# Half of the exchange of probabilities issued from SyncE, y's stores behind it in program order, and the last tile's sums of y put off

## The chip, the cores and the metric
One core of a Trainium2 chip. The time is device microseconds of one execution, the median of several runs; 1285.63 us for the kernel before. A profiled execution gives the trace; its own time is given beside it.

## The reference
Three stages follow each other over 4608 tokens of width 512. Names in brackets are those of the kernel.

```python
# 1. attention in chunks of 64 tokens, 8 heads of 64
p = exp(scores - max(scores)); p /= sum(p) + 1e-9      # scores = scale * qc @ kc.T   [sc, p]
x = p @ vc                                             # [x], split into [xh] + [xl]
# 2. FFN, 512 -> 2048 -> 512
h = x @ w_in; g = h * cos(h); y = g @ w_out            # [h], [gh]+[gl], [y]
# 3. FFN, 512 -> 1024 -> 512
h2 = y @ w_in2; s = h2 * softmax(h2)
ln = (s - mean(s)) / sqrt(var(s) + 1e-6) * g_ln
out = ln @ w_out2                                      # [o]
```

Inputs are float32; w_in, w_out, w_in2 and w_out2 arrive as 64-bit floats and are converted on the chip.

## The kernel before
Float32 products are made of three products of rounded halves (hi x hi, lo x hi, hi x lo), so operands are kept in pairs such as xh and xl, whi and wlo.

**Steps.** Stage 2 runs over 9 tiles of 512 tokens and 16 slices of the hidden width: 144 steps. A step n has 12 matmuls `h<-...` of slice n and 12 matmuls `y<-...` of slice n - 2. Steps 34 to 127 are written out in one order for every engine by `step(n)`; between their fixed parts stand slots ("e", "p1", "y", "a1", "d1", "a2", "d2", "p2") into which tables put the other work: p slots are for TensorE, a for ScalarE (ACT), d for VectorE (DVE).

**Attention inside the steps.** While tile t is worked on, the attention of tile t + 1 is made in two units of 256 tokens, the first begun two steps ahead of the tile's own steps, the second eight steps later. The table `exchanged` places a unit's parts by step and slot: DVE transposes q and k (`qt`, `kt`), TensorE makes the scores (`sc<-kt,qt`), DVE takes maximum, difference, sum and quotient, ACT the exponential. Then the probabilities have to be transposed in 64 x 64 blocks: DVE transposes 32 x 32 blocks (`ptr<-p`, line 545) and 16 DMAs of 32 KB put the blocks into their places (`ptb<-ptr`, line 552). This is the exchange; its DMAs are issued by GpSimd (POOL). TensorE then multiplies with v (`x<-ptb,vi`), at the end of the unit's step 8, ahead of the `h` matmuls of step 9, and `att_x` splits x into xh and xl.

**Weights of stage 3.** They are converted inside the steps too, by the pieces that `conv_at`, `blk_sum`, `keep` and `keep_out` place: loads `st<-in_moe_w...`, conversion in `z` (one buffer), and stores to DRAM (`w2f<-z`, `w2_..`).

**y.** At a tile's end y is moved out of PSUM (`ye<-y`), four sums of its quadrants are formed (`ts`, `sum_y`; stage 3's first product is a Strassen-Winograd one with seven products), and six DMAs `yd<-ye`, `yd<-ts` store both (`store_y`). `load_y(i)` loads pair i (256 tokens) again as `yr`, `split_y` makes `yh` (ACT) and `yl` (DVE) of it. Loads `yr`, `ye`, `ts` and the weights' loads share a pool "st" of two buffers.

**Stage 3** takes 18 pairs. The first three are mixed into the end of stage 2; from pair `EARLY` = 3 on a loop is written out in order: pair i's products `h2` (seen as `h<-whi,yh`), the softmax and the norm of pair i - 1, DVE transposes `bt`, 16 DMAs `lt<-bt` per tile, the split into `lh` and `ll`, and the products `o<-whi,lh` for 128 tokens at a time.

**What sets the order.** TensorE, ACT and DVE follow the written order in steps 34 to 127 and in the last loop. On SyncE (SP) only calls through the wrapper `sync` can be kept in program order, and only in the first 24 steps, where `in_order_loads` is true; elsewhere a scheduler puts SP's DMAs in the order in which it expects their operands.

Of the kernel before, what the change touches and what calls it, by code (L numbers as in the profile page):

```python
# [11 lines left out]
F32 = mybir.dt.float32  # L12
# [17 lines left out]
def kernel(  # L30
# [12 lines left out]
    nc = tc.nc  # L43
# [4 lines left out]
    P = 128  # L48
# [182 lines left out]

    def load_w2in(g):
        t = sp_.tile([P, 1024], U64, tag="st", name="st")
        nc.sync.dma_start(out=t, in_=w_in2[g * P:(g + 1) * P, :])
        raw["in2", g] = t

    def load_w2out(g):

        t = sp_.tile([P, 1024], U64, tag="st", name="st")
        for c in range(4):  # L240
            nc.sync.dma_start(
                out=t[32 * c:32 * (c + 1)].rearrange("p (e m) -> p e m", e=2),
                in_=w_out2.rearrange("(c q p) m -> c p q m", c=4, p=32)[c, :, 2 * g:2 * g + 2],
            )
        raw["out2", g] = t
# [4 lines left out]
    def conv(key, e, k):  # L250
        t = raw[key]
        w = t[:, HALVES[e]].bitcast(I32).rearrange("p (c w) -> p c w", w=2)
        low, high = w[:, :, 0], w[:, :, 1]
        if k == 0:
            if e == 0:
                wz[key] = zp.tile([P, 1024], I32, tag="z", name="z")
            act.activation(out=low, in_=low.bitcast(U32), func=AF.Copy, scale=2.0 ** -29)
            act.activation(out=wz[key][:, HALVES[e]].bitcast(F32), in_=high.bitcast(F32), func=AF.Abs)
            return
        z = wz[key][:, HALVES[e]]  # L260
        zf = z.bitcast(F32)
        if k == 1:
            dve.tensor_scalar(out=zf, in0=zf, scalar1=TINY, scalar2=None, op0=ALU.max)
            dve.tensor_scalar(
                out=z, in0=z, scalar1=3, scalar2=0x3FFFFFFF,
                op0=ALU.logical_shift_left, op1=ALU.bitwise_and,
            )
            return
        dve.scalar_tensor_tensor(
            out=z, in0=high, scalar=-(1 << 30), in1=z, op0=ALU.bitwise_and, op1=ALU.bitwise_or  # L270
        )
        dve.tensor_tensor(out=z, in0=z, in1=low, op=ALU.add)
        if key[0] == "in2" and e == 1:
            kk, x = key[1] % 2, key[1] // 2
            raw.pop(key)
            nc.sync.dma_start(
                out=w2f[kk][:, 1024 * x:1024 * (x + 1)], in_=wz.pop(key).bitcast(F32)
            )

# [1 line left out]

    def load_blk(kk):
        t = sp_.tile([P, 2048], F32, tag="st", name="wf")
        nc.sync.dma_start(out=t, in_=w2f[kk])
        blk[kk] = t, zp.tile([P, 1024], F32, tag="z", name="z"), sp_.tile([P, 2048], F32R, tag="st", name="wk")

    def blk_part(kk):
# [11 lines left out]
    def keep(kk, e, key, half):  # L299
        parts = blk[kk][2][:, 1024 * e:1024 * (e + 1)]  # L300
        split(blk_part(kk)[key], parts[:, HALVES[0]], parts[:, HALVES[1]], half=half)
        if half == 1:
            nc.sync.dma_start(
                out=w2_dram[key].rearrange("p (x k c) -> p x k c", x=2, k=2)[:, :, kk],
                in_=parts.bitcast(F32).rearrange("p (x c) -> p x c", x=2),
            )

    def keep_out(g, e, half):
        parts = raw["out2", g].bitcast(F32R)
        hi, lo = parts[:, 0:1024], parts[:, 1024:2048]  # L310
        src, sl = wz["out2", g].bitcast(F32)[:, HALVES[e]], HALVES[e]
        mul = gcol[:, 2 * g + e:2 * g + e + 1]
        if half == 0:
            act.activation(out=hi[:, sl], in_=src, func=AF.Copy, scale=mul)
            return
        dve.scalar_tensor_tensor(
            out=lo[:, sl], in0=src, scalar=mul, in1=hi[:, sl].bitcast(F32), op0=ALU.mult, op1=ALU.subtract
        )
        if e == 1:
            raw.pop(("out2", g)), wz.pop(("out2", g))  # L320
            nc.sync.dma_start(out=w2_dram[g], in_=parts.bitcast(F32))

    def fetch_w2(key):
        hi, lo = wtile(F32R, "whi"), wtile(F32R, "wlo")
# [212 lines left out]
    def att_pt(i):  # L537
        p = pr.pop(i)
        x = UNITS[i][1] // 2 * HU
        if i >= EXCH:  # L540

            t = work(i, (4, x, 32), "t", "ptr")
            o = work(i, (4, x, 32), "t", "ptb")
            tc.keep_in_program_order(
                nc.vector.transpose(
                    out=t.rearrange("p g x s -> p x g s"),
                    in_=p.rearrange("p x r (h s) -> p x (r h) s", s=32),
                )
            )
            for g in range(4):  # L550
                for c in range(4):
                    nc.gpsimd.dma_start(  # L552
                        out=o[32 * g:32 * (g + 1), c].rearrange("p x s -> p (x s)"),
                        in_=t[32 * c:32 * (c + 1), g].rearrange("p x s -> p (x s)"),
                    )
            ptb[i] = o
            return
        if small(i):
            t = ps_h.tile([P, x, P], F32, tag="h", name="pt")
        else:  # L560
            t = ps_a.tile([P, x, P], F32, tag="a", name="pt")
        for y in range(x):
            pe.transpose(out=t[:, y], in_=p[:, y].rearrange("p r k -> p (r k)"), identity=ident)
        pt[i] = t
# [125 lines left out]
    def mm_out(n):  # L690
# [17 lines left out]
                pe.matmul(out=o, lhsT=wb, rhs=a, start=False, stop=last)  # L708
        if last and not PIN <= n + LAG < END:
            evac_y(j, f)  # L710
            if f == NF - 1:
                for e in range(4):
                    sum_y(j, e)
                store_y(j)
# [2 lines left out]

    def load_part(j):
        t = sp_.tile([P, KD, T], F32, tag="st", name="yp")
        nc.sync.dma_start(out=t.rearrange("p m t -> p (m t)"), in_=y_part[j])  # L720
        parts[j] = t

    ye = {}
# [1 line left out]
    def evac_y(j, f, half=None):  # L725
# [17 lines left out]
            return  # L743
        yps.pop(j), ye.pop(j)
        if f < NF - 1:
            nc.sync.dma_start(out=y_part[j], in_=s.rearrange("p m t -> p (m t)"))
            return

        ys[j] = s, sp_.tile([P, 8, 256], F32, tag="st", name="ts")
# [13 lines left out]
    def store_y(j):  # L763
        s, ts = ys.pop(j)
        for p in range(2):
            dst = y_dram[j][p].rearrange("p (x t) -> p x t", t=P)
            sl, sr = slice(p * P, (p + 1) * P), slice(256 + p * P, 256 + (p + 1) * P)
            nc.sync.dma_start(out=dst[:, 0:4], in_=s[:, :, sl])
            nc.sync.dma_start(out=dst[:, 4:6], in_=s[:, 2:4, sr])
            nc.sync.dma_start(out=dst[:, 6:14], in_=ts[:, :, sl])  # L770


    NPAIR = NI // 2
# [23 lines left out]
    if True:  # L797
# [70 lines left out]
        def load_next_v(i):  # L868
# [7 lines left out]
            (6, "early", att_ptc), (6, "late", att_pv), (6, "late", load_next_v), (7, "early", att_x),  # L876
        )
        exchanged = (
            (0, "d1", lambda i: att_tr(i, "q")), (0, "d2", lambda i: att_tr(i, "k")),
            (2, "p1", att_qk), (2, "p1", load_next),  # L880
            (2, "d1", att_max), (3, "d1", att_sub), (3, "a2", att_exp),
            (4, "d1", att_sum), (5, "d1", att_mul), (5, "d2", att_pt),
            (8, "p2", att_pv), (8, "p2", load_next_v),
            (9, "e", lambda i: att_x(i, 0)), (9, "e", lambda i: att_x(i, 1)),
        )
# [14 lines left out]
        for i in range(SUB, NU):  # L900
# [3 lines left out]
            elif j == 2:  # L904
                place(i, NF + (0 if o == 0 else NB - 1), wide)
            else:
                place(i, j * NF - NF + (-2 if o == 0 else 6), exchanged)

        def plan(n, when, what):
            att.setdefault((n, when), []).append((lambda i: what(), NU))  # L910
# [5 lines left out]
        for t in (2, 3):  # L916
            o = NF * t
            for x in range(2):
                plan(o + 5, "p2", lambda g=2 * x + t - 2: load_w2in(g))
            conv_at(("in2", t - 2), ((o + 6, "a2"), (o + 7, "d2"), (o + 8, "d2"), (o + 7, "a1"), (o + 9, "d2"), (o + 10, "d2")))  # L920
            conv_at(("in2", t), ((o + 12, "a2"), (o + 12, "d2"), (o + 13, "d1"), (o + 13, "a1"), (o + 13, "d2"), (o + 16, "d1")))
        for t in (4, 5):
            o, kk = NF * t, t - 4
            plan(o + 5, "p2", lambda kk=kk: load_blk(kk))
# [10 lines left out]
        for t in (6, 7):  # L935
# [2 lines left out]
                g = 2 * (t - 6) + x  # L938
                plan(o + 5, "p2", lambda g=g: load_w2out(g))
            g = 2 * (t - 6)  # L940
            conv_at(("out2", g), ((o + 6, "a2"), (o + 7, "d2"), (o + 8, "d2"), (o + 7, "a1"), (o + 9, "d2"), (o + 10, "d2")))
            conv_at(("out2", g + 1), ((o + 12, "a2"), (o + 12, "d2"), (o + 13, "d1"), (o + 13, "a1"), (o + 13, "d2"), (o + 16, "d1")))
            for x, n0, wa, wd in ((0, 12, "a1", "d1"), (1, 16, "a2", "d2")):
                for e in range(2):
                    plan(o + n0, wa, lambda g=g + x, e=e: keep_out(g, e, 0))
                    plan(o + n0, wd, lambda g=g + x, e=e: keep_out(g, e, 1))
# [211 lines left out]
        W2_STEPS = (2, 3, 5, 8, 9, 9, 10, 10, 11, 12)  # L1158
        late_w = [(w, g) for g in range(NB // 2, NF // 2) for w in ("in", "out")]

        SLOTS = "e", "p1", "y", "a1", "d1", "a2", "d2", "p2"

        def step(n):
            if n == PIN:
# [29 lines left out]
                    plan(n + d, when, lambda j=j: store_y(j))  # L1194

        for n in range(NSTEP + LAG + 1):
            in_order_loads[0] = n < NF + NB
            ordered[0] = False
            if PIN <= n < END:
                step(n)  # L1200
# [34 lines left out]
            rest = n - NSTEP + NF  # L1235
            if rest == 3:
                load_y(0)
            elif rest == 4:
                split_y(0)
            for key, when in zip(BLOCKS + tuple(range(NF2 // 2)), (3, 3, 5, 5, 6, 7, 7, 13, 13, 15, 15)):  # L1240
# [6 lines left out]


        LAG2 = 7
        load_y(EARLY + 1, nc.gpsimd)  # L1250
        ordered[0] = True
        for i in range(EARLY, NI // 2 + (LAG2 + 1) // 2 + 1):
            p, t = i - 1, 2 * i - LAG2
# [43 lines left out]
                blocks32(p, 0)  # L1297
            if new:
                pair_sum(i, 1)
            if i == EARLY:  # L1300
                split_y(i + 1)
            if old:
                blocks32(p, 1)
                if p % 2:
# [2 lines left out]
            if new:  # L1307
                pair_mm(i, 2)
            half_o(t + 1, 0)
            if EARLY < i and i + 1 < NPAIR:  # L1310
                split_y(i + 1)
            if new:
                pair_sum(i, 2)
# [4 lines left out]
            half_o(t + 1, 1)  # L1318
            if new:
                pair_sum(i, 3)  # L1320
            if i + 2 < NPAIR:
                load_y(i + 2)

# [26 lines left out]
```

## Time and profile before

| | before |
|---|---|
| median of 3 runs (lowest to highest) | 1285.63 us (1285.53 to 1288.3) |
| the profiled execution's own time | 1284.95 us |
| its span in the trace | 1283.2 us |
| mean granted TensorE clock | 0.992 |
| PE (TensorE) busy | 1246.1 us, 97% |
| DVE busy | 957.9 us, 75% |
| ACT busy | 834.5 us, 65% |
| POOL busy | 122.4 us, 10% |

TensorE is busy for 97% of the span; the other engines have room on the average. A change can gain by closing TensorE's gaps, 37 us in all, and it loses by opening new ones. Matmuls are pipelined: each 128x512 matmul is shown with 0.39 us, but they start 0.227 us apart.

### The profile page before, as it was taken

The numbers are of one execution on the slowest core, as the hardware profiler recorded it, in microseconds if no ns is written. First come the engines' busy times: TensorE is split into PE (matmuls) and PEld (weight loads), VectorE is DVE, ScalarE is ACT, GpSimd is POOL, SyncE is SP. The second block draws the span as 40 slices with busy tenths as digits, with TensorE's granted clock in tenths as the row PEclk, the third lists the DMA queues.
The fourth block names the chain that finished last, engine by engine and source line by source line (L and its number), as shares of the span: only waits on it lengthen the run. The fifth ranks groups of instructions, "written<-read, shape, count | busy, mean of one in ns | idle before, by whom it ended". The sixth has DMA issues, their size and how long they took to land.

```text
span 1283.2 us, 20464 instructions
## 1 busy us (share of the span) xinstructions
PE 1246.1 (97%) x7556; PEld 1008.9 (79%) x7556; DVE 957.9 (75%) x1556; ACT 834.5 (65%) x1243; POOL 122.4 (10%) x272
## 2 busy tenths in 40 slices
PE   5899999999999999999999999999999999999998
PEld 4667778888878878878878878888878888888886
DVE  5887989687777777777778878757788777777761
ACT  5777876576656666656667767657756656656552
POOL 0000000020120220120121122000000000000000
PEclk9999999999999999999999999999999999999999
DMA  8952344343352343543563461380475443554224
GB/s 240 218 118 84 113 132 108 81 148 62 73 160 55 65 133 94 127 124 90 129 148 66 117 148 42 115 299 29 144 203 150 119 119 103 136 143 124 68 63 109
DMA packets 247940, 153.95 MB, mean 120 GB/s; under 512 B 180000, under 2 KB 220448, under 8 KB 246048
## 3 DMA queue, kind: packets, MB, share of 16 engines
q1 hardware_dynamic: 241456, 145.30, 43.5%
q0 software_dynamic: 6288, 7.22, 2.3%
q8 instruction: 59, 0.97, 0.3%
q14 instruction: 41, 0.34, 0.1%
q10 hardware_dynamic: 96, 0.13, 0.0%
HBM read 85.73 MB, written 41.68 MB: 99 GB/s over the span
## 4 chain that ended last, share of the span: by engine, by line
PE 72%; DVE 10%; ACT 8%; DMA 4%; POOL 3%; issue 2%; SPq 1%; ACTq 0%; POOLq 0%; DVEq 0%
PE h L105 34%; PE y L105 21%; PE o L105 13%; POOL ptb L552 3%; DMA ptb<-ptr 3%; DVE z L105 2%; DVE r L105 2%; ACT r L105 2%; PE x L105 2%; PE sc L105 1%; DVE gl L105 1%; ACT kt L105 1%; ACT hs L105 1%; DMA yr<-yd 1%; ACT whi L105 1%
## 5 line engine op out<-in xcount | busy, mean ns | idle before, releaser
L105 ACT ACTIVATE r<-r 128x512 f32<-128x512 f32 x288 | 181.8, 631 | 144.0 <-DVE r L105 138.2
L105 PE MATMUL h<-xh,whi 128*128 128x512 f32 x576 | 230.4, 400 | 2.0 <-ACT xh L105 1.4
L105 PE MATMUL h<-xh,wlo 128*128 128x512 f32 x576 | 226.4, 393 | 0.0
L105 PE MATMUL h<-xl,whi 128*128 128x512 f32 x576 | 225.8, 392 | 0.0
L105 PE MATMUL y<-gl,whi 128*128 128x512 f32 x544 | 212.7, 391 | 0.5 <-DVE gl L105 0.3
L105 PE MATMUL y<-gh,whi 128*128 128x512 f32 x544 | 211.9, 392 | 0.8 <-ACT gh L105 0.7
L105 PE MATMUL y<-gh,wlo 128*128 128x512 f32 x544 | 211.9, 390 | 0.0
L105 DVE SCALAR_TENSOR_TENSOR r<-kt,hs 128x512 f32<-128x512 int32 x144 | 99.0, 687 | 88.3 <-ACT kt L105 85.7
L552 POOL DMA_DIRECT2D ptb<-ptr x192 | 94.5, 500 | 708.3 <-DVE r L105 309.3
L105 DVE SCALAR_TENSOR_TENSOR hs<-r,hs 128x512 f32<-128x512 f32 x136 | 92.8, 682 | 59.6 <-ACT r L105 59.3
L105 ACT ACTIVATE hs<-h 128x512 f32<-128x512 f32 x144 | 85.0, 591 | 77.1 <-PE h L105 68.9
L105 PEld LDWEIGHTS h<-xh,whi 128*128 128x128 f32 x576 | 108.8, 189 | 27.8 <-issue 2.5
L105 PEld LDWEIGHTS h<-xl,whi 128*128 128x128 f32 x576 | 108.8, 189 | 23.8 <-issue 1.4
L105 PEld LDWEIGHTS h<-xh,wlo 128*128 128x128 f32 x576 | 108.8, 189 | 23.5 <-issue 0.4
L105 PEld LDWEIGHTS y<-gh,whi 128*128 128x128 f32 x544 | 101.8, 188 | 23.9 <-ACT gh L105 1.9
L105 PEld LDWEIGHTS y<-gl,whi 128*128 128x128 f32 x544 | 102.1, 188 | 23.2 <-DVE gl L105 2.4
L105 PEld LDWEIGHTS y<-gh,wlo 128*128 128x128 f32 x544 | 102.1, 188 | 21.3 <-DVE wlo L105 0.3
L105 PE MATMUL o<-whi,lh 128*128 128x512 f32 x288 | 112.4, 390 | 1.3 <-ACT os L105 1.3
L105 PE MATMUL o<-wlo,lh 128*128 128x512 f32 x288 | 112.3, 390 | 0.0
L105 PE MATMUL o<-whi,ll 128*128 128x512 f32 x288 | 112.1, 389 | 0.0
L105 DVE TENSOR_TENSOR gl<-hs,gh 128x512 fp32r<-128x512 f32 x136 | 93.0, 684 | 10.4 <-ACT gh L105 10.3
L105 PE MATMUL h<-whi,yh 128*128 128x512 f32 x252 | 98.6, 391 | 1.6 <-ACT yh L105 1.6
(108 smaller groups left out, 2077.9 us busy)
## 6 DMA issues: line engine op xcount, KB each, us to landing
lt<-bt SPq DMA_DIRECT2D x144, 128.0 KB
yr<-yd SPq DMA_DIRECT2D x17, 896.0 KB
yd<-ts SPq DMA_DIRECT2D x18, 512.0 KB
out<-os SPq DMA_DIRECT2D x142, 64.0 KB
vi<-in_v SPq DMA_DIRECT2D x64, 128.0 KB
qi<-in_q SPq DMA_DIRECT2D x224, 32.0 KB
ki<-in_k SPq DMA_DIRECT2D x224, 32.0 KB
ptb<-ptr POOLq DMA_DIRECT2D x192, 32.0 KB, 1.7
```

What stands on the lines that cost most here:

```text
L105: ins = getattr(self.engine, name)(*args, **kwargs)
L552: nc.gpsimd.dma_start(out=o[32 * g:32 * (g + 1), c].rearrange("p x s -> p (x s)"), in_=t[32 * c:32 * (c + 1), g].rearrange("p x s -> p (x ...
```

## The change
Four things are changed together.

1. Of an exchange's 16 DMAs the 8 of the groups g < 2 are issued by SP, the other 8 by POOL as before.
2. In steps 34 to 127 SP keeps program order: `in_order_loads` is true there, and all stores and loads in them go through `sync`.
3. The table of slots: k's transpose goes one step later, the scores from slot p1 to p2 of step 2, the maximum from d1 to d2. The product with v of a tile's first unit (`first_x`) goes from the end of step 8 to slot p1 of step 9, that is behind the 12 `h` matmuls of step 9; the second unit's (`second_x`) stays. Pieces of the weights' conversion go up to some steps later, and slot p2 stands ahead of a2 and d2.
4. The last tile's four sums and its `store_y` go from the end of stage 2 to behind pair 3's last sums; pair 4's load goes from POOL, behind the loop of steps, to SP, right behind pair 3's load; pair 4's `split_y` goes behind the second transpose `bt` and the `ll` of that iteration.

```diff
@@ att_pt
-                    nc.gpsimd.dma_start(
+                    (sync if g < 2 else nc.gpsimd).dma_start(
                         out=o[32 * g:32 * (g + 1), c].rearrange("p x s -> p (x s)"),
@@ load_w2in, load_w2out, conv, load_blk, keep, keep_out, load_part, evac_y, store_y
-            nc.sync.dma_start(out=dst[:, 0:4], in_=s[:, :, sl])
+            sync.dma_start(out=dst[:, 0:4], in_=s[:, :, sl])
...
@@ mm_out
-            if f == NF - 1:
+            if f == NF - 1 and j < NJ - 1:
                 for e in range(4):
                     sum_y(j, e)
                 store_y(j)
@@ exchanged
-            (0, "d1", lambda i: att_tr(i, "q")), (0, "d2", lambda i: att_tr(i, "k")),
-            (2, "p1", att_qk), (2, "p1", load_next),
-            (2, "d1", att_max), (3, "d1", att_sub), (3, "a2", att_exp),
+            (0, "d1", lambda i: att_tr(i, "q")), (1, "d2", lambda i: att_tr(i, "k")),
+            (2, "p2", att_qk), (2, "p2", load_next),
+            (2, "d2", att_max), (3, "d1", att_sub), (3, "a2", att_exp),
             (4, "d1", att_sum), (5, "d1", att_mul), (5, "d2", att_pt),
+        )
+        first_x = (
+            (9, "p1", att_pv), (9, "p1", load_next_v),
+            (9, "a1", lambda i: att_x(i, 0)), (9, "d1", lambda i: att_x(i, 1)),
+        )
+        second_x = (
             (8, "p2", att_pv), (8, "p2", load_next_v),
             (9, "e", lambda i: att_x(i, 0)), (9, "e", lambda i: att_x(i, 1)),
@@ place
-                place(i, j * NF - NF + (-2 if o == 0 else 6), exchanged)
+                place(i, j * NF - NF + (-2 if o == 0 else 6), exchanged + (second_x if o else first_x))
@@ conv_at, as one example of four
-            conv_at(("in2", t), ((o + 12, "a2"), (o + 12, "d2"), (o + 13, "d1"), (o + 13, "a1"), (o + 13, "d2"), (o + 16, "d1")))
+            conv_at(("in2", t), ((o + 13, "a1"), (o + 13, "d1"), (o + 13, "d2"), (o + 13, "a2"), (o + 14, "d2"), (o + 16, "d1")))
@@
-        SLOTS = "e", "p1", "y", "a1", "d1", "a2", "d2", "p2"
+        SLOTS = "e", "p1", "y", "a1", "d1", "p2", "a2", "d2"
@@ the loop of steps
-            in_order_loads[0] = n < NF + NB
+            in_order_loads[0] = n < NF + NB or PIN <= n < END
...
+            elif rest == 16:
+                load_y(EARLY + 1)
@@ the loop of pairs
-        load_y(EARLY + 1, nc.gpsimd)
...
-            if i == EARLY:
-                split_y(i + 1)
             if old:
                 blocks32(p, 1)
...
-            if EARLY < i and i + 1 < NPAIR:
+            if i + 1 < NPAIR:
                 split_y(i + 1)
...
             if new:
                 pair_sum(i, 3)
+            if i == EARLY:
+                for e in range(4):
+                    sum_y(NJ - 1, e)
+                store_y(NJ - 1)
             if i + 2 < NPAIR:
                 load_y(i + 2)
```

On SP, around the stores of tile 2's y (`yd_82`), before:

```order
L105 DMA ki<-in_k 32x8x32 x16
L276 DMA w2f_115<-z 128x1024
L768 DMA yd_82<-ye 128x4x128
L769 DMA yd_82<-ye 128x2x128
L768 DMA yd_82<-ye 128x4x128
L769 DMA yd_82<-ye 128x2x128
L770 DMA yd_82<-ts 128x8x128 x2
L234 DMA st<-in_moe_w_in 128x1024 x2
```

And after, where `ptb<-ptr` are the 8 DMAs of the tile's first exchange:

```order
L105 DMA w2f_115<-z 128x1024
L105 DMA qi<-in_q 32x8x32 x16
L105 DMA ki<-in_k 32x8x32 x16
L105 DMA ptb<-ptr 32x256 x8
L105 DMA yd_82<-ye 128x4x128
L105 DMA yd_82<-ye 128x2x128
L105 DMA yd_82<-ts 128x8x128
L105 DMA yd_82<-ye 128x4x128
L105 DMA yd_82<-ye 128x2x128
L105 DMA yd_82<-ts 128x8x128
L105 DMA st<-in_moe_w_in 128x1024 x2
```

The 8 DMAs of the exchange now stand on SP ahead of all six stores of y and of the weights' load; the store of z stands ahead of the loads of q and k, where it stood behind them.

On TensorE, around the first unit's product with v (`x<-ptb,vi`), before:

```order
L105 MATMUL y<-gh,whi 128x512
L105 MATMUL y<-gl,whi 128x512
L105 MATMUL y<-gh,wlo 128x512
L105 MATMUL x<-ptb,vi 64x64 x32
L105 MATMUL h<-xh,whi 128x512
L105 MATMUL h<-xl,whi 128x512
L105 MATMUL h<-xh,wlo 128x512
```

And after:

```order
L105 MATMUL h<-xh,whi 128x512
L105 MATMUL h<-xl,whi 128x512
L105 MATMUL h<-xh,wlo 128x512
L105 MATMUL x<-ptb,vi 64x64 x32
L105 MATMUL y<-gh,whi 128x512
L105 MATMUL y<-gl,whi 128x512
L105 MATMUL y<-gh,wlo 128x512
```

The product has gone behind the 12 `h` matmuls that it stood ahead of.

On DVE, in the iteration of pair 3 (`h_8992`, `h_8993` are pair 2's rows, `h_92..` pair 3's, `yl` pair 4's lower half), before:

```order
L105 STREAM_TRANSPOSE bt<-h_8992 128x32x32
L105 TENSOR_TENSOR h_9243<-h_9262,h_9243 128x512
L105 TENSOR_TENSOR h_9242<-h_9262,h_9243 128x512
L105 TENSOR_TENSOR yl<-yr,yh 128x1024
L105 TENSOR_TENSOR yl<-yr,yh 128x768
L105 STREAM_TRANSPOSE bt<-h_8993 128x32x32
L105 TENSOR_TENSOR ll<-lt,lh 128x1024
```

And after:

```order
L105 STREAM_TRANSPOSE bt<-h_8992 128x32x32
L105 TENSOR_TENSOR h_9233<-h_9252,h_9233 128x512
L105 TENSOR_TENSOR h_9232<-h_9252,h_9233 128x512
L105 STREAM_TRANSPOSE bt<-h_8993 128x32x32
L105 TENSOR_TENSOR ll<-lt,lh 128x1024
L105 TENSOR_TENSOR yl<-yr,yh 128x1024
L105 TENSOR_TENSOR yl<-yr,yh 128x768
```

`yl` has gone behind the second transpose and `ll`. The last tile's four sums `ts` stood 17 to 23 rows ahead of this `yl`; now they stand 9 to 11 rows behind it.

## Rows read from the trace of the kernel before

**Rows 1.** Waits of PE, 240 to 940 us: total us, times, longest.

```profile
PE x L105 <- DMA ptb<-ptr: 10.0, 6, 2.8
```

**Rows 2.** PE's timeline: start us, us, engine line operation out<-in.

```profile
283.76 1.16 PE L105 MATMUL x<-ptb,vi 64*64 64x64 f32 x64
284.85 0.50 PE L105 MATMUL h<-xh,whi 128*128 128x512 f32 x1
...
376.15 0.75 PE L105 MATMUL x<-ptb,vi 64*64 64x64 f32 x6
...
473.35 0.34 PE L105 MATMUL x<-ptb,vi 64*64 64x64 f32 x6
...
568.38 0.72 PE L105 MATMUL x<-ptb,vi 64*64 64x64 f32 x6
...
664.06 0.68 PE L105 MATMUL x<-ptb,vi 64*64 64x64 f32 x6
...
757.88 0.33 PE L105 MATMUL x<-ptb,vi 64*64 64x64 f32 x4
760.94 0.50 PE L105 MATMUL h<-xh,whi 128*128 128x512 f32 x1
```

**Rows 3.** POOL's timeline at one exchange.

```profile
364.39 1.47 POOL L552 DMA_DIRECT2D ptb<-ptr  x3 [37.12 <-DVE ptr L545]
366.13 6.36 POOL L552 DMA_DIRECT2D ptb<-ptr  x13 [0.27 <-issue]
```

**Rows 4.** Chain of waits, the same stretch: start us, us, what.

```profile
372.00 7.54 DMA ptb<-ptr
```

**Rows 5.** The tile ptb, 410 to 426 us, a second unit.

```profile
DMA to landing us min/median/max: 1.6/1.7/1.7
```

**Rows 6.** SP's timeline around that exchange.

```profile
343.48 7.79 SPq L105 DMA_DIRECT2D ki<-in_k  x16
351.37 0.40 SPq L276 DMA_DIRECT2D w2f<-z  x1
...
369.26 0.99 SPq L770 DMA_DIRECT2D yd<-ts  x2
370.42 5.64 SPq L234 DMA_DIRECT2D st<-in_moe_w_in  x2
```

**Rows 7.** DVE's timeline, the same unit.

```profile
338.62 0.69 DVE L105 SCALAR_TENSOR_TENSOR hs<-r,hs 128x512 f32<-128x512 f32 x1 [1.36 <-ACT r L105]
...
344.46 0.69 DVE L105 CUSTOM_DVE_ANT_0 z<-st,z 128x1024 uint16<-128x1024 uint16 x1
...
362.62 1.24 DVE L545 STREAM_TRANSPOSE ptr<-p 128x1024 f32<-128x1024 f32 x1
...
368.54 0.69 DVE L105 TENSOR_TENSOR ts<-ye,ts 128x512 f32<-128x512 f32 x1
```

**Rows 8.** PE's timeline, the scores of that unit.

```profile
339.40 1.16 PE L105 MATMUL sc<-kt,qt 64*64 64x64 f32 x64
```

**Rows 9.** Chain of waits around 316 us: twelve `y` matmuls of a step.

```profile
316.39 2.72 PE y L105 x12
```

**Rows 10.** PE's timeline where pair 4 begins.

```profile
948.49 0.39 PE L105 MATMUL o<-whi,ll 128*128 128x512 f32 x1
950.49 0.50 PE L105 MATMUL h<-whi,yh 128*128 128x512 f32 x1 [1.62 <-ACT yh L105]
...
955.32 0.63 PE L105 MATMUL o<-whi,lh 128*128 128x512 f32 x1
```

**Rows 11.** Windows: us, busy PE, PEld, DVE, ACT, POOL, PEclk, DMA share, GB/s.

```profile
952.00:956.00 4.00, 4.00 (x12) 3.15 (x12) 4.00 (x7) 1.91 (x2) 0.00 (x0) 0.60 0.93 340
```

**Rows 12.** Chain of waits, pair 4's load.

```profile
938.39 10.97 DMA yr<-yd
```

**Rows 13.** DVE's timeline, pair 4's lower half.

```profile
950.47 2.09 DVE L105 TENSOR_TENSOR yl<-yr,yh 128x1024 fp32r<-128x1024 f32 x2 [3.06 <-ACT yh L105]
```

**Rows 14.** ACT's timeline: pair 2's exponential, pair 5's upper half.

```profile
936.80 1.15 ACT L105 ACTIVATE e<-h,nm 128x1024 f32<-128x1024 f32 x1 [2.76 <-DVE nm L105]
...
967.47 1.77 ACT L105 ACTIVATE yh<-yr 128x1024 fp32r<-128x1024 f32 x2
```

**Rows 15.** Waits of SP, 870 to 930 us.

```profile
SPq L325 <- PE h L105: 26.5, 1, 26.5
```

More of the change, by code (lines that the diff above doesn't have):

```diff
@@ L233, in load_w2in @@
         t = sp_.tile([P, 1024], U64, tag="st", name="st")
-        nc.sync.dma_start(out=t, in_=w_in2[g * P:(g + 1) * P, :])
+        sync.dma_start(out=t, in_=w_in2[g * P:(g + 1) * P, :])
         raw["in2", g] = t
@@ L240, in load_w2out @@
         for c in range(4):
-            nc.sync.dma_start(
+            sync.dma_start(
                 out=t[32 * c:32 * (c + 1)].rearrange("p (e m) -> p e m", e=2),
@@ L275, in conv @@
             raw.pop(key)
-            nc.sync.dma_start(
+            sync.dma_start(
                 out=w2f[kk][:, 1024 * x:1024 * (x + 1)], in_=wz.pop(key).bitcast(F32)
@@ L283, in load_blk @@
         t = sp_.tile([P, 2048], F32, tag="st", name="wf")
-        nc.sync.dma_start(out=t, in_=w2f[kk])
+        sync.dma_start(out=t, in_=w2f[kk])
         blk[kk] = t, zp.tile([P, 1024], F32, tag="z", name="z"), sp_.tile([P, 2048], F32R, tag="st", name="wk")
@@ L302, in keep @@
         if half == 1:
-            nc.sync.dma_start(
+            sync.dma_start(
                 out=w2_dram[key].rearrange("p (x k c) -> p x k c", x=2, k=2)[:, :, kk],
@@ L320, in keep_out @@
             raw.pop(("out2", g)), wz.pop(("out2", g))
-            nc.sync.dma_start(out=w2_dram[g], in_=parts.bitcast(F32))
+            sync.dma_start(out=w2_dram[g], in_=parts.bitcast(F32))
     def fetch_w2(key):
@@ L719, in load_part @@
         t = sp_.tile([P, KD, T], F32, tag="st", name="yp")
-        nc.sync.dma_start(out=t.rearrange("p m t -> p (m t)"), in_=y_part[j])
+        sync.dma_start(out=t.rearrange("p m t -> p (m t)"), in_=y_part[j])
         parts[j] = t
@@ L745, in evac_y @@
         if f < NF - 1:
-            nc.sync.dma_start(out=y_part[j], in_=s.rearrange("p m t -> p (m t)"))
+            sync.dma_start(out=y_part[j], in_=s.rearrange("p m t -> p (m t)"))
             return
@@ L767, in store_y @@
             sl, sr = slice(p * P, (p + 1) * P), slice(256 + p * P, 256 + (p + 1) * P)
-            nc.sync.dma_start(out=dst[:, 0:4], in_=s[:, :, sl])
-            nc.sync.dma_start(out=dst[:, 4:6], in_=s[:, 2:4, sr])
-            nc.sync.dma_start(out=dst[:, 6:14], in_=ts[:, :, sl])
+            sync.dma_start(out=dst[:, 0:4], in_=s[:, :, sl])
+            sync.dma_start(out=dst[:, 4:6], in_=s[:, 2:4, sr])
+            sync.dma_start(out=dst[:, 6:14], in_=ts[:, :, sl])
     NPAIR = NI // 2
@@ L919 @@
                 plan(o + 5, "p2", lambda g=2 * x + t - 2: load_w2in(g))
-            conv_at(("in2", t - 2), ((o + 6, "a2"), (o + 7, "d2"), (o + 8, "d2"), (o + 7, "a1"), (o + 9, "d2"), (o + 10, "d2")))
-            conv_at(("in2", t), ((o + 12, "a2"), (o + 12, "d2"), (o + 13, "d1"), (o + 13, "a1"), (o + 13, "d2"), (o + 16, "d1")))
+            conv_at(("in2", t - 2), ((o + 7, "a2"), (o + 8, "d2"), (o + 9, "d2"), (o + 8, "a2"), (o + 10, "d1"), (o + 12, "d1")))
+            conv_at(("in2", t), ((o + 13, "a1"), (o + 13, "d1"), (o + 13, "d2"), (o + 13, "a2"), (o + 14, "d2"), (o + 16, "d1")))
         for t in (4, 5):
@@ L940 @@
             g = 2 * (t - 6)
-            conv_at(("out2", g), ((o + 6, "a2"), (o + 7, "d2"), (o + 8, "d2"), (o + 7, "a1"), (o + 9, "d2"), (o + 10, "d2")))
-            conv_at(("out2", g + 1), ((o + 12, "a2"), (o + 12, "d2"), (o + 13, "d1"), (o + 13, "a1"), (o + 13, "d2"), (o + 16, "d1")))
-            for x, n0, wa, wd in ((0, 12, "a1", "d1"), (1, 16, "a2", "d2")):
+            conv_at(("out2", g), ((o + 7, "a2"), (o + 8, "d2"), (o + 9, "d2"), (o + 8, "a2"), (o + 10, "d1"), (o + 12, "d1")))
+            conv_at(("out2", g + 1), ((o + 13, "a1"), (o + 13, "d1"), (o + 13, "d2"), (o + 13, "a2"), (o + 14, "d2"), (o + 16, "d1")))
+            for x, n0, wa, wd in ((0, 12, "a2", "d2"), (1, 16, "a2", "d2")):
                 for e in range(2):
```

## The prediction
> **What bounds the kernel now.** The busy shares come first: TensorE works for 97% of the span and the rest is some 37 us, so the time can fall only by closing TensorE's gaps. The waits of PE come next: from 240 to 940 us one releaser is left, the exchange of probabilities, 10.0 us in six waits [rows 1]. PE's timeline shows where [rows 2]. From the product with v of tile 2 (283.76) to that of tile 3 (376.15) nothing is in the way, and a tile takes 92.39 us. The next four distances are 97.20, 95.03, 95.68 and 93.82, which is 4.81, 2.64, 3.29 and 1.43 more. The last product takes 3.06 us from its start to the next `h` (757.88 to 760.94), where the first takes 1.09 (283.76 to 284.85): 1.97 more. Together 14.14 us. That is above the 10.0 because the 64x64 matmuls also come in drops, as pieces land, with gaps too small for the list of waits.
>
> POOL's timeline and the chain of waits tell why. The 32x32 transpose ends at 363.86 [rows 7]. POOL issues 16 DMAs in 8.1 us, 364.39 to 372.49, 0.49 us each [rows 3]. The one issued at 372.00 takes 7.54 us to land, until 379.54 [rows 4], while in an undisturbed exchange a landing takes 1.7 us [rows 5]. What disturbs it is on SP: the stores of `ts` from 369.26 and two loads of 1 MB from 370.42 [rows 6]. The first DMAs are ahead of these, the last ones are not, and PE wants the product at 376.15.
>
> Then the window where pair 4 begins. Behind `o` at 948.49 the next matmul could start 0.23 later, at 948.72; it starts at 950.49, held by `yh` [rows 10]. The `h` block of 12 takes from 950.49 to 955.32, 4.83 us, where twelve matmuls take 2.72 [rows 9]; the granted clock in 952 to 956 is 0.60 of full speed, which is the lower level of 1.2 GHz for most of it, behind a stretch in which PE stood still [rows 10, 11]. The first three `o` matmuls are slow too, 0.45 more. Excess: 1.77 + 2.11 + 0.45 = 4.33 us. Its cause is pair 4's load, issued at 938.39 and 10.97 us on its way [rows 12].
>
> **Part 1 and 2, the exchange and SP's order.** With 8 DMAs on each of two engines the last is issued 8 x 0.49 = 3.9 us behind the transpose, near 368.3, which is ahead of where `ts` is summed (368.54 to 369.23, [rows 7]), and the stores of y and the loads of 1 MB now stand behind the exchange on SP. The last piece lands near 368.3 + 1.7 = 370. For this SP must be free at 363.9. In the new order the store of z stands ahead of the loads of q and k; z is ready at 345.15, when the row that ends its work does [rows 7], and 32 loads at 0.49 (16 took 7.79, [rows 6]) end near 361. Free by 3 us, and what is wanted only later than 370 has 6 us more.
>
> The Trainium skill (DMA: Bandwidth & Descriptors, "Issuing engines are not separate DMA queues") speaks against this part: starting DMAs from several engines saves only the sequencers' time for issuing, usually small beside the DMA itself. Here the rows differ from the "usually": issuing takes 8.1 us and a landing 1.7 [rows 3, 5]. Where the rule holds nonetheless, the result is rival A.
>
> **Part 3, the slots.** The product with v moves behind 12 `h` matmuls, 2.72 us [rows 9], so PE wants it at 376.15 + 2.72 = 378.87, some 8 us behind the landing. All of the 14.14 us goes; I take it whole, with 10.0 as the lower end [rows 1, 2]. What is late next: x must be split before the `h` of the tile's first step, and a half of a step less remains for the split. A clean product ends in 1.1 us and a second unit's has the same split in the slots behind it, so I expect none of it back. k's transpose loses room: it would follow `hs` (338.62 + 0.69) and take 1.24, to 340.55, and the scores, at 339.40 so far, go 2.72 later to 342.12 [rows 7, 8]: 1.5 us are left. The maximum goes along with the scores.
>
> The pieces of the weights' conversion move with them, and here the change adds waits. ACT writes z, of which there is one buffer, and z's store can now stand behind the second unit's 8 DMAs on SP, 3.9 us at 0.49. Behind the waiting instruction on ACT stand a step's `r` and `gh`, which PE waits for. No row shows this wait. Its lower end is 0, as z's stores leave earlier too (at 351.37 before, though z was ready at 345.15, [rows 6, 7]). Its upper end: if a half step of 2.72 us hides part of the 3.9 us, 1.2 us are left, in six tiles 7 us. I take 0.6 us, as SP issued that store within an idle stretch before.
>
> **Part 4, the tail.** Pair 4's load stands right behind pair 3's on SP, over 10 us earlier, and SP has 26.5 us of waiting for PE in that stretch [rows 15], so it holds up nothing. It is then no load that ends the wait but the order on DVE. DVE was free at 950.47 - 3.06 = 947.41 [rows 13]. Now a transpose and an `ll`, 1.24 + 1.2 = 2.4 us, stand ahead of `yl`, and the four sums of 0.69 each [rows 7], 2.75 us, are gone from ahead of it. ACT's exponential waited 2.76 us for DVE just there [rows 14], so most of the 2.75 is passed on, but not with certainty all. `yl` starts between 947.06 and 949.81, and PE gets its first half 1.28 later (950.47 to 951.75 before), between 948.34 and 951.1. PE wants it at the third matmul, 949.17. Remaining wait 0 to 1.9 us; I take 0.5, as the exponential's wait is nearly the whole 2.75. Gain 4.33 - 0.5 = 3.83, and with so short a gap I expect the clock to stay up.
>
> What is given back: pair 5's load on SP now stands behind the last `ts` stores. `yl` from 948.1, 2.1 us, four sums of pair 3 and four `ts` of 0.69 each: 955.7, then three issues of 0.5: 957.2. With 10.97 us on its way, the only row [rows 12], it lands at 968.2. ACT took it at 967.47 [rows 14], and would take it up to 3.8 us earlier now, as PE runs ahead by that. The queue is emptier there than in the row. 0 to 3 us; I take 0.7, as ACT has some lead on PE.
>
> **Sum.** -14.14 (exchange) - 3.83 (tail) + 0.6 (z) + 0.7 (pair 5) = -16.7 us. The profiled execution took 1284.95 (span 1283.2 and 1.75 around it): 1268.3. The median of the runs is 0.68 above that execution, so 1269.0. By the ends alone: exchange 10.0 and tail 4.33 - 1.9, and 3 back for pair 5, and z at nothing, gives 1276; all gained and nothing back gives 1284.95 - 18.47 + 0.68 = 1267.2. The likeliest case's own range is 1266.5 to 1273.
>
> **Rivals.**
> A. The split between two engines brings nothing, since all DMAs share the same transfers, and only the later slot counts: each tile gains at most 2.72. 2.72 + 2.64 + 2.72 + 1.43 + 1.97 = 11.5, and the time is 1271.6. For it: the last landing's 7.54 us are transfer, not issue [rows 4]. Against it: pieces issued before 369 are ahead of the disturber [rows 3, 6].
> B. The exchange's gain is half lost to ACT's waits for z and for loads that SP, now in program order, issues later: the 7 us above. 1269.0 + 6.5 = 1275.5. For it: one buffer of z, and ACT's position in each step is fixed. Against it: ACT is busy for 65% only.
> C. The change doesn't do what it says: SP's half is held by something ahead of it in program order (k's loads, which wait for the transpose that goes a step later), so the exchange ends 2.7 us later and eats the new slot; and pair 5's load takes back 3 of the tail's 3.8. About 1284. For it: 32 loads right ahead of the exchange. Against it: 3 us of room, and 6 beyond it.
> D. Slower: SP's issues become the bound. A first exchange's SP half must start by 378.87 - 3.9 - 1.7 = 373.3 to be in time; from 345.15 there are 28.1 us for 32 loads, so it decides from 0.88 us an issue. POOL's and SP's rows show 0.49, but the 1 MB loads 2.8 each [rows 3, 6]. At 1.0 us an issue the exchange is 32 x 1.0 - 28.1 = 3.9 us late in six products, 23 us in place of 14: 1284.95 + 23 - 14.1 - 3.1 + 0.7 = 1291.
>
> **Chances and range.** Forecast 0.62, A 0.12, B 0.12, C 0.08, D 0.06. A measurement of this kernel can tell 0.2%, 2.6 us, from no change. Forecast, A and B are faster, with C's better part: 0.87. The rest of C is the same: 0.07. D is slower: 0.06. The range 1265.5 to 1277.5 takes in A and B and leaves out C and D, and some of B's tail.
>
> **What would show it.** The list of PE's waits from 240 to 940 has no `ptb<-ptr` row, or one under 1 us; the distances of a tile's first products are near 92.4 for each tile; landings of `ptb` stay under 3 us; SP's `ptb` issues start within 1 us of the transpose. If these landings are short and the distances are still above 94, ACT's waits for z or `st` in the steps 7 to 14 of a tile are the cause (B). If PE waits for `ptb<-ptr` at the later slot, see when SP issued its half: late is C or D, at once and slowly landed is A. In the tail PE waits for `yl` and no longer for `yh`, under 2 us, with a clock near full speed in that block; a wait for `yh` some 20 us later would be pair 5's load. The forecast is wrong if the sum of the five tile distances falls by less than 8 us.

## The result and the profile after

The changed kernel takes 1267.65 us in the median of 4 runs (1267.08 to 1268.27), the kernel before 1285.58 of 4: a ratio of 0.9857, 95% interval 0.984 to 0.9874. The forecast was 1269.0 us. The profiled execution took 1267.08 us, 17.87 less than that of before; the forecast's sum was 16.7 less. Its span is 18.1 us shorter (1283.2 and 1265.1); the rest is time outside the span, 1.75 us before and 1.98 after.

The page of the changed kernel gives span, busy time and share of each engine:

```profile
span 1265.1 us, 20549 instructions
PE 1239.9 (98%) x7556; PEld 1005.0 (79%) x7556; DVE 959.0 (76%) x1556; ACT 834.2 (66%) x1243; POOL 74.9 (6%) x175
```

The waits of PE from 240 to 940 us (us in total, times, longest):

```profile
PE h L105 <- DVE yl L105: 0.2, 1, 0.2
```

The `ptb<-ptr` wait of [rows 1] is gone. PE's timeline at the tiles' first products with v:

```profile
286.18 1.04 PE L105 MATMUL x<-ptb,vi 64*64 64x64 f32 x55
...
378.56 0.64 PE L105 MATMUL x<-ptb,vi 64*64 64x64 f32 x28
...
747.89 1.16 PE L105 MATMUL x<-ptb,vi 64*64 64x64 f32 x64
748.99 0.50 PE L105 MATMUL y<-gh,whi 128*128 128x512 f32 x1
```

From 286.18 to 378.56 a tile takes 92.38 us, as before. The next four take 747.89 - 378.56 = 369.33, 92.33 each, where [rows 2] have 381.73: 12.40 us less. The last product takes 1.10 to the next matmul, where it took 3.06: 1.96 less. Together 14.36 us; the forecast was 14.14.

SP's timeline at the exchange of [rows 3, 6], and POOL's:

```profile
344.44 0.34 SPq L105 DMA_DIRECT2D w2f<-z  x1
344.83 8.27 SPq L105 DMA_DIRECT2D qi<-in_q  x16
353.14 9.06 SPq L105 DMA_DIRECT2D ki<-in_k  x16
363.65 5.01 SPq L105 DMA_DIRECT2D ptb<-ptr  x8
368.77 1.07 SPq L105 DMA_DIRECT2D yd<-ye  x2
369.94 0.44 SPq L105 DMA_DIRECT2D yd<-ts  x1
370.42 2.02 SPq L105 DMA_DIRECT2D yd<-ye  x2
372.48 0.97 SPq L105 DMA_DIRECT2D yd<-ts  x1
375.03 2.22 SPq L105 DMA_DIRECT2D st<-in_moe_w_in  x2
```

```profile
364.12 2.45 POOL L552 DMA_DIRECT2D ptb<-ptr  x5 [41.62 <-DMA ki<-in_k]
366.73 1.49 POOL L552 DMA_DIRECT2D ptb<-ptr  x3 [0.16 <-issue]
```

SP is free at 362.2, 1.5 us ahead of its 8 pieces (a piece is one of the exchange's 16 DMAs), and both halves are issued by 368.7, as forecast. The landings of the half that POOL issues (the trace has none for SP's half):

```profile
DMA to landing us min/median/max: 1.7/1.7/1.8
```

The loads of 1 MB start at 375.03; before, the first started at 370.42. That last line is easy to read past, and the experiments show that the gain hangs on it.

In the tail, PE's timeline where pair 4 begins, the window there (us, busy PE, PEld, DVE, ACT, POOL, PEclk, DMA share, GB/s) and the chain of waits:

```profile
933.82 0.39 PE L105 MATMUL o<-whi,ll 128*128 128x512 f32 x1
...
934.88 0.50 PE L105 MATMUL h<-whi,yl 128*128 128x512 f32 x1 [0.21 <-DVE yl L105]
...
937.31 0.39 PE L105 MATMUL o<-whi,lh 128*128 128x512 f32 x1
```

```profile
934.00:938.00 4.00, 3.79 (x17) 2.75 (x17) 4.00 (x8) 0.00 (x0) 0.00 (x0) 1.00 0.00 0
```

```profile
934.88 2.60 PE h L105 x10
937.47 2.72 PE o L105 x12
```

From the last `o` to the next block's `o` it is 3.49 us; [rows 10] have 6.83. The clock stays at 1.00 and the 12 `o` take 2.72, so the 0.45 of slow ones is saved too: 3.79 us. The wait that is left is for `yl`, as forecast, and `yh` has none. Pair 5's load on SP, its `yh` on ACT, and ACT's wait for z's store in the steps:

```profile
942.08 1.22 SPq L778 DMA_DIRECT2D yr<-yd  x1
```

```profile
950.99 1.77 ACT L105 ACTIVATE yh<-yr 128x1024 fp32r<-128x1024 f32 x2
```

```profile
ACT z L105 <- DMA w2f<-z: 4.4, 2, 2.3
```

The `yh` has no wait in front of it; the wait for z is new, and PE shows no gap of it.

### The profile page after: what moved, and what is told of

Read it like the earlier page. It is cut to its first block, busy times and chain, and to the rows that moved or that the text cites. A ratio compares the mean times of both kernels' runs of the same rounds, so it can differ in the third digit from the quotient of the medians.

```text
span 1265.1 us, 20549 instructions
## 1 busy us (share of the span) xinstructions
PE 1239.9 (98%) x7556; PEld 1005.0 (79%) x7556; DVE 959.0 (76%) x1556; ACT 834.2 (66%) x1243; POOL 74.9 (6%) x175
## 4 chain that ended last, share of the span: by engine, by line
PE 83%; DVE 7%; ACT 5%; issue 3%; SPq 1%; DMA 1%; POOL 0%; ACTq 0%; DVEq 0%; POOLq 0%
PE h L105 40%; PE y L105 27%; PE o L105 13%; DVE z L105 2%; PE x L105 2%; PE sc L105 1%; DVE r L105 1%; ACT whi L105 1%; SPq L1114 1%; DVE p L105 1%; DVE h L105 1%; ACT r L105 1%; SPq L105 1%; DVE s L105 0%; DMA raw<-in_moe_w_in 0%
## 5 line engine op out<-in xcount | busy, mean ns | idle before, releaser
L105 DVE SCALAR_TENSOR_TENSOR r<-kt,r 128x512 f32<-128x512 int32 x144 | 98.7, 685 | 0.7
L105 ACT ACTIVATE gh<-hs 128x512 fp32r<-128x512 f32 x136 | 84.4, 620 | 22.2 <-DVE hs L105 22.1
```

The costliest lines, as they stand in the source:

```text
L105: ins = getattr(self.engine, name)(*args, **kwargs)
```

## The experiments

Three things in the change can each help the exchange: the split over two engines, SP's program order, and the later slot. The forecast put the split and the order together and added the slot as room. The first runs take them away one by one. All runs have the rest of the change, unless said otherwise, and were timed in rounds with the kernel before.

**All 16 on POOL** (split off).

```diff
-                    (sync if g < 2 else nc.gpsimd).dma_start(
+                    nc.gpsimd.dma_start(
```

> All 16 DMAs of each exchange on POOL again, the rest of the change kept: SP's program order, the later slot, the tail. Theory (pieces that are issued behind 369 us collide with y's stores; either remedy, earlier issue or later slot, takes most of the wait): the last piece is issued near 372 and lands up to 7.5 us later, near 379.5, against a product that is wanted at 378.6; by the tile distances of before less 2.72 us a slot, 2.1 and 0.6 us come back in two tiles: 1267.65 + 2.7 = 1270.3 us, landings of ptb up to 7 us. Rival 1 (the split is what counts, the slot hides little): some 12 us come back, 1280. Rival 2 (the split brings nothing, the slot is all): 1267.6 and landings as in the changed kernel.

Measured 1267.22 us (1265.51 to 1267.27). The time of rival 2 came, but not its landings: the last pieces take up to 4.1 us. The theory's 1270.3 was 3.1 us too high. The landings in this exchange, and SP's timeline:

```profile
DMA to landing us min/median/max: 1.7/1.7/4.1
```

```profile
369.47 0.36 SPq L105 DMA_DIRECT2D yd<-ts  x1
369.87 1.99 SPq L105 DMA_DIRECT2D yd<-ye  x2
371.91 1.00 SPq L105 DMA_DIRECT2D yd<-ts  x1
375.74 1.85 SPq L105 DMA_DIRECT2D st<-in_moe_w_in  x2
```

The pieces still meet y's stores, but the loads of 1 MB come only at 375.74. So with program order and the later slot the split isn't needed, and program order is what moved the loads: with the scheduler's order they start at 370.70 again (the slot alone, below).

**The old slot** (split and order kept).

```diff
-    place(i, j * NF - NF + (-2 if o == 0 else 6), exchanged + (second_x if o else first_x))
+    place(i, j * NF - NF + (-2 if o == 0 else 6), exchanged + second_x)
```

> The first unit's product with v back in its place at the end of step 8, ahead of the h matmuls; split, program order and tail kept. Theory: the last piece lands near 370, the product is wanted near 376: no wait, 1267.6 us within 1, tile distances 92.3. Rival 2 (the later slot is what took the wait away): the waits of before come back, up to 2.72 us a tile, 11.5 in all: 1279.

Measured 1267.21 us (1266.56 to 1268.18), no wait for `ptb`. As expected: with the split and program order the slot isn't needed either.

**Order alone** (both edits above).

> All 16 DMAs of the exchange on POOL and the old slot for the product with v; SP's program order, the other tables and the tail kept. New theory, from the run with 16 on POOL: program order alone moves the disturber, the two loads of 1 MB start at 375.7 us in place of 370.4; the last piece is issued at 372.2 and lands within 3 to 4 us, near 376, when the product is wanted: waits under 1 us a tile, 1267.5 to 1270 us. Rival (order alone isn't enough, either the split or the later slot is needed): at least half of the 14.1 us is back, 1275 to 1281.

Measured 1267.08 us (1265.01 to 1267.82); PE waits once, 0.9 us. As expected. The moved tables and the tail are kept here; "alone" is meant among the three.

**The slot alone** (16 on POOL; SP in the scheduler's order).

```diff
-            in_order_loads[0] = n < NF + NB or PIN <= n < END
+            in_order_loads[0] = n < NF + NB
```

> 16 on POOL and SP in the scheduler's order as before; the new slots and tables and the tail kept. The scheduler puts four of y's stores early and the loads of 1 MB near 370 us again. New theory (program order moves the disturber): landings of 7 us are back, until 379.5 against 379 wanted in the late slot: 2.1 and 0.6 us in two tiles by the distances of before, 1268.5 to 1271. Rival (the slot by itself is as good): 1267.2 to 1267.7 and short landings.

Measured 1269.16 us (1266.99 to 1269.64). Landings of up to 8.8 us are back, and PE waits 1.7 us in two products: the slot hides nearly all of a collision that still takes place, as expected.

**The split and the slot, without order** (only the diff of the run above).

> The split and the new tables kept, SP in the scheduler's order, which puts SP's 8 pieces between y's stores but ahead of ts and of the 1 MB loads. Theory: pieces land by 371, no wait for ptb; 1267 to 1269 us. Rival (without program order SP's half comes late, behind loads of q and k or a store that waits): waits for ptb of over 2 us in several tiles, 1272 to 1290.

Measured 1268.54 us (1268.12 to 1268.97), no wait for `ptb`. The time is as expected, but the run doesn't show that the split closes the wait by itself. The slot is kept, and SP's timeline shows that the loads of 1 MB have moved too, from 370.70 in the run before to here:

```profile
374.14 2.26 SPq L105 DMA_DIRECT2D st<-in_moe_w_in  x2
```

With SP's 8 pieces in its queue the scheduler has put y's stores in another order. The split without the slot and with the loads near 370 us was not run.

**None of the three** (slot alone, with the old slot), and then **only y's order** put into it: the six stores of y and the loads of 1 MB (`load_w2in`, `load_blk`, `load_w2out`) go through a wrapper of their own and keep order among themselves; nothing else on SP does.

```diff
+    in_order_y = [False]
+    ysync = InOrder(nc.sync, in_order_y)
...
-            sync.dma_start(out=dst[:, 0:4], in_=s[:, :, sl])
+            ysync.dma_start(out=dst[:, 0:4], in_=s[:, :, sl])
...
+            in_order_y[0] = PIN <= n < END
```

> All three remedies of the exchange off: 16 on POOL, SP in the scheduler's order, the old slot for the product with v; the other tables and the tail kept. Theory (any one of the three closes the wait, so without all of them it is back): landings of 7 us and more, waits for ptb as before, 1267.1 + 14.1 = 1281 us, 1279 to 1282.5. Rival (the moved tables, that is later scores and weights' pieces, took part of it away): 1269 to 1276.

> As the run without all three, with one thing given back: the six stores of y and the loads of 1 MB keep program order among themselves on SP (the second half's ye stores wait for the first ts), nothing else does. Theory (the disturber is the loads of 1 MB, and the order matters because it moves them from 370.5 to some 375 us): loads start near 375, landings 4 to 6 us at most, waits for ptb under 2 us in all, 1267 to 1269.5 us. Rival (the stores disturb as much as the loads, or the whole queue's order is needed): 1274 to 1281.

Measured 1286.44 us (1283.39 to 1288.52, 10 runs) and 1267.49 us (1265.98 to 1268.85); the kernel before 1288.11 in these rounds. The first is above the 1279 to 1282.5 expected, by 4 us; the kernel before is 2.5 above its first rounds too, and the runs of both scatter by 5 to 7 us. In the profiled executions, from the first product that waits to the last, it takes 386.74 us (375.74 to 762.48) where the kernel before takes 381.73 [rows 2]. PE's list explains 1.3 of these 5.0 (11.3 us of waits in place of 10.0). The granted clock goes with the rest: it falls behind such waits, before in one tile, here in four. One of before's windows, then two of this run's:

```profile
380.00:384.00 4.00, 4.00 (x66) 3.48 (x59) 3.79 (x4) 1.63 (x3) 0.00 (x0) 0.65 0.37 119
```

```profile
476.00:480.00 4.00, 3.07 (x61) 2.79 (x62) 1.86 (x3) 1.02 (x1) 0.00 (x0) 0.50 0.07 16
480.00:484.00 4.00, 4.00 (x14) 3.16 (x13) 1.19 (x1) 0.41 (x1) 0.00 (x0) 0.68 0.63 140
```

0.50 is the lower level, 1.2 GHz; in the changed kernel the clock is 1.00 in all three windows. The second time is as expected, and it is the run that settles the cause. SP's timeline and the chain of waits without the three:

```profile
368.85 0.99 SPq L105 DMA_DIRECT2D yd<-ts  x2
370.01 1.25 SPq L105 DMA_DIRECT2D st<-in_moe_w_in  x1
...
375.36 0.35 SPq L105 DMA_DIRECT2D st<-in_moe_w_in  x1
```

```profile
371.59 8.04 DMA ptb<-ptr
379.77 1.61 PE x L105 x58
```

With y's order alone, SP's timeline, the landings in this exchange and the product with v:

```profile
368.23 0.36 SPq L105 DMA_DIRECT2D yd<-ts  x1
368.63 1.99 SPq L105 DMA_DIRECT2D yd<-ye  x2
370.66 0.99 SPq L105 DMA_DIRECT2D yd<-ts  x1
374.52 1.77 SPq L105 DMA_DIRECT2D st<-in_moe_w_in  x2
```

```profile
DMA to landing us min/median/max: 1.7/1.7/4.1
```

```profile
375.11 1.16 PE L105 MATMUL x<-ptb,vi 64*64 64x64 f32 x64
```

Of the two loads of 1 MB one goes into the buffer of `ye`, the other into that of `ts`. Without order all of `ye` is stored near 356 to 359, so one buffer is free, and the first load starts right behind the `ts` stores at 370.01, amid the exchange; SP then waits 4.0 us for a `ts` store before the second. Pieces issued from 371 on take 8 us. With order the last `ye` stores stand behind the first `ts`, SP waits for them, and the first load starts only at 374.52. The stores are then wholly inside the exchange, and the pieces take 4.1 us at most. It is the first load that did the harm, by far more than the stores.

**The place in SP's queue, made worse.** SP's half of a first unit's exchange goes behind the stores and the loads (slot a2 of its step 7).

```diff
+        first_x = (
+            (7, "a2", att_half),      # SP's 8 DMAs; POOL's 8 stay in att_pt
```

> The 8 DMAs that SP issues of a first unit's exchange are put behind y's stores and the two loads of 1 MB on SP (slot a2 of the unit's step 7 in place of d2 of step 5), all else as changed. Theory (the place on SP ahead of stores and loads is what counts): stores until 373.5, loads until 377.3, 8 issues until 382.3, landing by 384 to 390 against 378.6 wanted: 5.5 to 11 us of wait in each of six products with v, 1300 to 1334 us. Rival (a place in SP's queue hardly matters as the transfers share the same engines): within 5 us of 1267.6.

Measured 1309.04 us (1305.41 to 1311.76). PE waits for `ptb` 28.0 us, in five products, the longest 8.7; SP issues the half from 377.1, until 385. The time is in the range expected; of the products, three wait 6.7 to 8.7 us, two some 2, and tile 2's not at all. The tile distances hold the whole loss of 41.4 us; it is more than the waits, and the mean granted clock is 0.977, where the changed kernel has 0.994.

**All 16 on SP.**

```diff
-                    (sync if g < 2 else nc.gpsimd).dma_start(
+                    sync.dma_start(
```

> All 16 DMAs of each exchange on SP, ahead of y's stores in program order, none on POOL. Theory (what counts is that no piece is behind the stores, not that two engines issue): SP issues 16 in about 9.5 us from 363.7, the last lands near 375, ahead of 378.6: no wait of PE for ptb, 1267.6 us within 1. Rival 1 (the split over two engines is needed): the exchange ends 4 to 5 us later and PE waits for it in the first units, 1270 to 1285. Rival 3 (SP in program order is near its limit): y's stores and the loads behind them go 4.5 us later, ACT waits for z and st grow and PE shows gaps outside x, 1270 or more.

Measured 1299.63 us (1298.77 to 1301.45); the theory fell here, and rival 3 came, far above the 1270 that it named. The waits of PE and the largest of ACT for DMAs from 240 to 940 us:

```profile
PE y L105 <- ACT gh L105: 7.3, 6, 2.3
PE x L105 <- DMA ptb<-ptr: 6.6, 6, 1.9
PE y L105 <- DVE gl L105: 2.8, 9, 0.3
PE h L105 <- DVE xl L105: 2.0, 2, 1.2
PE x L105 <- issue: 0.6, 1, 0.6
```

```profile
ACT wk L105 <- DMA w_s<-wk: 17.9, 2, 9.2
ACT z L105 <- DMA w2f<-z: 16.4, 2, 8.7
...
ACT st L105 <- DMA st<-in_moe_w_out: 11.5, 2, 6.1
```

Stores of z and wk now stand behind 10 us of issues, ACT waits for them, and the steps' own work on ACT comes late. The waits for `ptb` are all of second units, whose slot was not moved. PE's list of waits shows 19 of the 32 us; where the rest lies is open.

**The tables of before** (split, order and tail kept; slots, scores and the weights' pieces back).

```diff
-            (0, "d1", lambda i: att_tr(i, "q")), (1, "d2", lambda i: att_tr(i, "k")),
-            (2, "p2", att_qk), (2, "p2", load_next),
+            (0, "d1", lambda i: att_tr(i, "q")), (0, "d2", lambda i: att_tr(i, "k")),
+            (2, "p1", att_qk), (2, "p1", load_next),
...
-            conv_at(("out2", g), ((o + 7, "a2"), (o + 8, "d2"), ...
+            conv_at(("out2", g), ((o + 6, "a2"), (o + 7, "d2"), ...
```

> Split, program order and the tail, with the tables of before (scores, conversion pieces, slots, product with v at the end of step 8). Theory: z's store stands right ahead of SP's half and z is ready a step earlier than that, so the exchange is still clean: 1267 to 1269 us. Rival B (the tables were moved because ACT and SP would wait for z and its store): ACT's waits for z and SP's for z grow, PE shows gaps at gh or x, 1272 to 1290.

Measured 1274.2 us (1272.92 to 1274.75). Rival B came, at 6.5 us; the theory fell. The exchange is clean, but ACT waits for the loads that order has moved: the wait shown here was 6.9 us in the kernel before and is 0.7 in the changed one. ACT's largest such wait, then PE's list:

```profile
ACT st L105 <- DMA st<-in_moe_w_out: 11.8, 2, 6.0
```

```profile
PE sc L105 <- DVE xl L105: 3.6, 2, 1.8
PE h L105 <- DVE xl L105: 1.5, 2, 1.0
```

So, as far as the trace tells, the later steps of the conversion are the price of the loads' later start, and they belong to the order. They were put back together with the scores and the slots; a run with them alone was not made.

**The tail alone**, on the kernel before (part 4 of the diff).

> The kernel before with part 4 alone (the last tile's sums and stores put off, pair 4's load on SP, its split behind the second transpose). Theory: the parts add, PE waits 0.2 us for yl in place of 1.6 + 0.5, and the clock stays up: 3.8 us less than the kernel before of the same rounds, near 1282. Rival (the tail's gain needs the earlier part's SP order): 0 to 1.5 us less.

Measured 1285.42 us (1281.75 to 1289.55, 10 runs) against 1288.11: 2.7 us less, ratio 0.9983, interval 0.9965 to 1.0001. By time alone it is at the edge of what can be told. The trace tells it: PE waits 0.2 us for `yl`, none for `yh`, as with the whole change, and from the last `o` to the next block's `o` it is 3.46 us (951.81 to 955.27), so the tail doesn't need the rest. The profiled execution shows little of it in its time, 1284.71 us against 1284.95, as its products with v took longer: 384.87 us from tile 3's to tile 7's, against 381.73.

**The split of pair 4 first** (order alone, with `yl` ahead of the second transpose).

```diff
+            if i == EARLY:
+                split_y(i + 1)
             if old:
                 blocks32(p, 1)
```

> Program order alone for the exchange (16 on POOL, old slot), the tail with pair 4's split ahead of the second transpose and ll, as it stood before, its load early. Theory (the load was what held the tail, the place of the split only decides 0.2 us): no wait for yl or yh where pair 4 begins, o waits under 0.3 us for ll; 1266.8 us, less than the measurement can tell from 1267.1. Rival (the place of the split is what closes the gap): PE waits over 1 us at o for ll, or at h, 1268 to 1270.

Measured 1267.11 us (1265.82 to 1268.04). The wait for `yl` is gone, and the time is that of the run it was made from, 1267.08. It was not the place of the split that held the tail. The chain before ran through the load (`yh` on ACT waits for it, [rows 12, 13]); the sums put off are kept in this run, so the load's part and theirs were not taken apart. None of these versions is faster than the changed kernel by what can be measured; program order with the moved tables and the tail does the same without the split and the slot.

## Why the prediction was right, and where not

- **The exchange.** Forecast -14.14, measured -14.36. That pieces behind 369 us meet a disturber, and that nothing of the wait stays, was right, and the steps named came as named: issued by 368.7, ahead of the disturber. Which of them does it was not right: the step "With 8 DMAs on each of two engines the last is issued ... near 368.3" was taken for what is needed. With 16 on POOL the last is issued at 372 and the time is the same. So the time fits although that step wasn't needed, and the fit is no proof of it. Of the three, program order alone suffices (1267.08), and of it the order of y's stores and the loads behind them (1267.49); the slot alone nearly does (1269.16). The split alone was not run.
- **What a wait costs.** The prediction puts the 4.1 us by which its 14.14 exceeds the list of waits down to matmuls that come in drops. Some 1.5 of it, by an estimate, are the clock behind tile 3's wait, 0.65 in 380 to 384 us: the product's last 58 matmuls take 1.86 us there and 1.05 in tile 4, and the first three `h` 1.35 in place of 0.68. In the run without the three it falls in four tiles. That fits with the gain in medians, 17.9 us here and up to 21.0 for versions of the same speed in the later rounds; the forecast had no term for it.
- **The rule on issuing engines** (Trainium skill, DMA: Bandwidth & Descriptors, "Issuing engines are not separate DMA queues") says that several issuing engines save only the time of issuing, usually small. The forecast set it aside, as issuing takes 8.1 us and a landing 1.7. What the Trainium skill says there of the gain held: 1267.22 us with one engine, 1267.65 with two. Its "usually small" did not hold, at 8.1 against 1.7 us. Issue time saved ahead of 376 us buys nothing where landings are short.
- **The row read too fast.** `370.42 5.64 ... st<-in_moe_w_in x2` of [rows 6] was taken as one disturber along with the stores. It is one load at 370 and one some 5 us later, each when SP finds its buffer free; the first was the harm. Rival D's "2.8 each" for these loads comes from the same reading and holds 4.0 us of SP's waiting.
- **Rival A** supposed that the slot hides 11.5 us by itself. The slot alone gave 1269.16, 2.4 us below A's 1271.6. It gained 16.6 us on the kernel before of its rounds, and the run without the three 1.7, so the slot hides some 15: A had priced it too low. But the change doesn't rest on it.
- **New waits of ACT**, forecast 0.6, measured none on PE. They exist (ACT waits 4.4 us for z's store) and are hidden. With the tables of before ACT waits for the loads instead, 11.8 us in two waits, and 6.5 us are lost, the price that B had.
- **D**, SP's limit, lay nearer than the forecast saw: 8 more issues for each exchange, and 32 us were lost. In PE's list the work that ACT and DVE finish late (`gh` and `gl`, 10.1 us) counts for more there than the exchange, 6.6.
- **The tail.** Forecast -3.83, measured -3.79, with 0.21 left of the wait for `yl` where 0.5 was taken.
- **Pair 5's load**, forecast 0.7 back, measured none: SP issued it at 942.08, ACT took `yh` at 950.99 without a wait. It landed in under 9 us, where the row taken for it, a load issued by POOL, had 10.97 [rows 12]; whether the emptier queue or the issuing engine made the difference isn't shown.

Exchange and tail as measured give 18.15, which is the span's 18.1. Against the forecast's 16.7 the new waits that did not come are 1.3 and the exchange 0.2; the time outside the span takes 0.2 back, which leaves the 17.87.

## What to carry to other kernels

When a small transfer lands late, ask which buffer's release started the large one that it meets, and whether that release can be put later; it may cost a few lines of order rather than a second issuing engine. A wait of TensorE can cost more than its length, since the clock may fall behind it; look at the granted clock there. A change made of several parts that each close the same gap says nothing of any one of them until they are taken away singly and together. And count what stands behind added issues on the same queue: a store that frees a single buffer can be dearer there than the transfer itself.

## What was not expected of the hardware

SP issued the same 32 KB pieces in 0.63 us each (8 in 5.01), POOL in 0.49 (5 in 2.45), so moving an issue to SP made it longer. The kernels with the collision scatter more, 1283.5 to 1290.9 us for the kernel before in the 19 runs of the last rounds, at mean granted clocks of 0.986 to 0.993, than order alone and y's order alone, 1265.0 to 1268.9 in 4 runs each at 0.991 to 0.996. The traces show falls of the clock behind waits for `ptb`, so part of the scatter is the clock; how large a part was not worked out.
